# A clamp and a small addition move from VectorE to GpSimd in an attention and gated-MLP kernel

## The chip, the cores and the metric

The kernel runs on one core of a Trainium2 chip. The metric is the device time of one execution in microseconds (us), as a median of runs. The core has five engines with a queue each: TensorE (PE; its weight loads are listed as PEld), VectorE (DVE), ScalarE (ACT), GpSimd (POOL) and SyncE (SP, which issues the transfers). Each engine takes its instructions in the order in which they stand in its queue; a semaphore holds an instruction until what it needs is done.

## The reference

```python
mask   = q_bucket[:, :, :, None] == k_bucket[:, :, None, :]   # sign bits of q @ proj, k @ proj (6 bits)
scores = np.where(mask, scale * q @ k^T, -1e9);  scores -= max(scores)
attn   = exp(scores);  attn = attn / (sum(attn) + 1e-9);  x = attn @ v      # 2 x 8 heads, 768 x 64
x = x as (1536, 512)
x = ((x @ w1) * (x @ w2) @ w3) @ w_out                        # first MLP, weights 512 x 1024, 1024 x 1024, 1024 x 512
out = (sigmoid(x @ w_gate) * (x @ w_val)) @ w_out2            # second MLP, 512 x 1536, 1536 x 512
```

q, k, v and proj come as float32; the seven weight matrices come as float64.

## The kernel before

Products are made of float32 operands split into a high and a low part: ScalarE rounds the high part, VectorE or GpSimd subtracts to get the low part, and TensorE does three matmuls for each product (`three`).

**Decode.** The float64 weights are turned into float32 on the chip, in 76 units of 128x512 values. `stage_next` issues the load of a unit (512 KB) from SP into a tile `st`. `decode` then takes the two 32-bit words of each value: ScalarE writes the magnitude of the high word, read as a float32, to `da` (L334) and a scaled low word to `dr` (L335); VectorE clamps the magnitude between two constants (L336), shifts and masks it (L337), puts the sign bit back (L338), and adds the low bits into the destination (L343, shown in the trace as a custom operation). The tiles `da` and `dr` have one buffer in each of two pools in turn during attention, and two buffers later.

**Attention.** 96 steps, six for each of 16 heads. In a step TensorE makes 128x768 scores (L466, L469); VectorE takes their negated maximum (L476, L477); ScalarE does the exponential and, as a by-product, the sum of the row, into one column of `su` (L487); TensorE transposes the result (L520), ScalarE and VectorE split it (L523, L524), and TensorE multiplies it with v (L537). When all six columns of `su` are there, `emit_rows` adds 1e-9 to them (L498), takes the reciprocal (L499), and sends the 128x6 values as a row to DRAM and back as a broadcast `rr` (two transfers from SP). GpSimd multiplies the head pair's output by it (`emit_scale`, L510). GpSimd also makes the splits of the next heads' q, k and v (`split`, L366 and L369).

**Filler.** Between the attention steps the kernel multiplies w3 by w_out into `wc` (`gen_fill`, L593) and starts the first MLP on the first 512 tokens (`gen_first`). Forty of the 76 decodes belong to these two. GpSimd makes the low halves of w_out (L588) and of the weights (`split_w`, L692).

**Order.** Everything up to here is collected first, and then `order_engines` writes out the order of each engine's queue by a list schedule: priorities from the step, a cost for each instruction, and a delay for each hop from engine to engine. For GpSimd the cost does not look at the operation:

```python
        if e == "Pool":
            return 60 + n * 2.3
...
            ("Pool", "Activation"): 75, ("Pool", "DVE"): 69, ("Pool", "PE"): 203}
```

For VectorE a tensor_scalar of n elements costs 69 + 0.52 n. Both in ns.

**The MLPs.** `moe` goes over 52 tiles of 512 tokens by 128 features: 24 matmuls into `pa` and `pb`, 12 into the accumulators `m`. The weights of the tile after next are split by ScalarE and GpSimd (`wah`, `wal`, `wbh`, `wbl`, L692), those of the second product by ScalarE and VectorE (`wth`, `wtl`). In the first 24 tiles the other 36 decodes run, one or two a tile. The order of this part is set by the framework's own scheduler, not by `order_engines`.

Of the kernel before, what the change touches and what calls it, by code (L numbers as in the profile page):

```python
# [16 lines left out]
ALU = mybir.AluOpType  # L17
# [6 lines left out]
F64_LO = 2.0 ** -15  # L24
F64_HI = 2.0 ** 17 - 2.0 ** -7
# [203 lines left out]
def lsh_attention_moe_moe2_kernel(  # L229
# [40 lines left out]
    dve = nc.vector  # L270
    pool = nc.gpsimd
# [6 lines left out]
    def f(ap):  # L278
        return ap.bitcast(F32)
# [30 lines left out]
    def stage_next():  # L310

        if units:
            dst, src = units.pop(0)
            alt[0] += 1
            other = late.get("mp") or (wp if "mw" not in late else dec)
            t = (other if alt[0] % 2 else dec).tile([P, CH], U64, tag="st", name="st", bufs=2)
            shp = dst.shape
            ld = sync.dma_start(out=t if len(shp) == 2 else t.rearrange("p (k f) -> p k f", k=shp[1]), in_=src)
            if "c0" in late and alt[0] == 4:
                Tiles.holds.append((ld.ins.name, late["c0"].name))  # L320
            staged.append((dst, t))

    def decode():


        stage_next()
        dst, t = staged.pop(0)
        w = t[:, :].bitcast(U32).rearrange("p (n t) -> p n t", t=2)
        lw, hw = w[:, :, 0], w[:, :, 1]
        alt[1] += 1  # L330
        tp, nb = (late["mp"], 2) if "mp" in late else (wp if "mw" not in late and alt[1] % 2 else dec, 1)
        a = tp.tile([P, CH], U32, tag="da", name="da", bufs=nb)
        r = tp.tile([P, CH], I32, tag="dr", name="dr", bufs=nb)
        act.activation(out=f(a), in_=f(hw), func=AF.Abs)  # L334
        act.activation(out=r, in_=lw, func=AF.Copy, scale=2.0 ** -29)  # L335
        dve.tensor_scalar(out=f(a), in0=f(a), scalar1=F64_LO, scalar2=F64_HI, op0=ALU.max, op1=ALU.min)  # L336
        dve.tensor_scalar(out=a, in0=a, scalar1=3, scalar2=0x3FFFFFFF, op0=ALU.logical_shift_left, op1=ALU.bitwise_and)  # L337
        dve.scalar_tensor_tensor(out=a, in0=hw, scalar=0xC0000000, in1=a, op0=ALU.bitwise_and, op1=ALU.bitwise_or)  # L338
        ai, ri = a.bitcast(I32), r
        if len(dst.shape) == 3:  # L340
            ai = ai.rearrange("p (k f) -> p k f", k=dst.shape[1])
            ri = ri.rearrange("p (k f) -> p k f", k=dst.shape[1])
        dve.tensor_tensor(out=dst.bitcast(I32), in0=ai, in1=ri, op=ALU.add)  # L343
# [135 lines left out]
    def emit_exp(g):  # L479
        h, t = divmod(g, NT)  # L480
        s = sc_t.pop(g)
        sm = sm_t.pop(g)
        if t == 0:
            su_t[h] = ap_.tile([P, NT], F32, tag="su", name=f"su{h}")
        e = ap_.tile([P, S], F32, tag="e", name=f"e{g}", bufs=3)
        e_t[g] = e
        act.activation(  # L487
            out=e.rearrange("p (a c) -> p a c", a=2), in_=s[:, :, :HS], func=AF.Exp,
            bias=sm[:, 1:2], scale=sm[:, 0:1], accum_out=su_t[h][:, t:t + 1],
        )  # L490
        if t == NT - 1:
            emit_rows(h)

    def emit_rows(h):

        su = su_t.pop(h)
        rs = ap_.tile([P, NT], F32, tag="rs", name=f"rs{h}")
        dve.tensor_scalar(out=su, in0=su, scalar1=1e-9, scalar2=None, op0=ALU.add)  # L498
        dve.reciprocal(out=rs, in_=su)  # L499
        row = drm.tile([1, S], F32, tag="row", name=f"row{h}")  # L500
        sync.dma_start(out=row.rearrange("o (p c) -> (o p) c", c=NT), in_=rs)
        if h % 2 == 0:
            rr_t[h // 2] = ap_.tile([P, S], F32, tag="rr", name=f"rr{h}", bufs=1)
        r0 = (h % 2) * D
        sync.dma_start(out=rr_t[h // 2][r0:r0 + D], in_=row.to_broadcast([D, S]))
# [49 lines left out]
    def gen_fill():  # L555
# [11 lines left out]
        for _ in range(3):  # L567
            stage_next()
        decode()
        decode()  # L570
        for i in range(NF1):
            t3 = [wp.tile([P, NF1, P], F32R, tag=f"t3{x}", name=f"t3{x}_{i}") for x in range(2)]
# [11 lines left out]
            for j in range(NF1):  # L584
                if i == 0:
                    decode()
                    act_copy(wo[0][:, j], wor[j])
                    pool.tensor_tensor(out=wo[1][:, j], in0=wor[j], in1=f(wo[0][:, j]), op=ALU.subtract)  # L588
                    yield
                elif i + 1 < NF1 and j in (2, 5):  # L590
                    decode()
                for n, (x, y) in enumerate(((0, 0), (0, 1), (1, 0))):
                    pe.matmul(acc, lhsT=t3[x][:, j], rhs=wo[y][:, j], start=(j == 0 and n == 0), stop=(j == NF1 - 1 and n == 2))  # L593
                if j % 2 == 1:
                    if j == NF1 - 1:
                        act_copy(wc[:, i], acc)
                    yield
# [327 lines left out]
```

## Time and profile before

| what | before |
|---|---|
| median of 3 runs | 856.51 us |
| lowest, highest | 855.91, 858.85 us |
| the profiled execution: time | 857.49 us |
| the profiled execution: span | 855.5 us |
| granted TensorE clock (share of full) | 0.996 |
| PE, DVE, ACT, POOL busy | 805.7, 592.3, 525.2, 283.5 us |

The span goes from the first to the last instruction; the time is that of the whole execution, 2 us more. Busy times are sums of an engine's instruction records. A record of TensorE, VectorE or ScalarE may overlap the next one of the same engine by a little, since the end of an instruction overlaps the start of the next.

### The profile page before, as it was taken

The page shows a single profiled execution, that of the slowest core. Times are in us where ns is not written, and L with a number is a line of the kernel's source. Part 1 is how long each engine was busy: PE and PEld are TensorE (multiplying, and loading weights), DVE is VectorE, ACT ScalarE, POOL GpSimd, SP SyncE. Part 2 cuts the span into 40 slices and gives each one's busy share as a digit, 9 for nine tenths or more (in the row PEclk, how much of TensorE's full clock was granted, in tenths as well). Part 3 has the DMA queues.
Part 4 walks back from the last instruction along what each step waited for, and adds up shares of the span by engine and source line. Part 5 has one row for each costly group of instructions (what it writes and reads, how often), then busy time and mean ns, then how long its engine had stood idle before and what let it go on. Part 6 is the DMA issues. An engine that isn't in the chain of part 4 may idle for free.

```text
span 855.5 us, 12210 instructions
## 1 busy us (share of the span) xinstructions
PE 805.7 (94%) x4272; PEld 681.2 (80%) x4272; DVE 592.3 (69%) x1059; ACT 525.2 (61%) x1024; POOL 283.5 (33%) x236
## 2 busy tenths in 40 slices
PE   4777999999979999999999999999999999999998
PEld 3656888889878889897788777778888888888886
DVE  5999999998889999999569999972222222222222
ACT  4778878887778988888347656663334433343331
POOL 1343323232325343227423342343333323333230
PEclk9999999999989999999999999999999999999999
DMA  7555555443334544323105433400000000010001
GB/s 223 150 172 173 147 135 128 123 105 99 84 110 104 161 112 124 81 59 109 49 10 172 162 124 128 144 1 1 1 0 26 26 1 0 1 50 1 0 1 49
DMA packets 44908, 71.54 MB, mean 84 GB/s; under 512 B 6128, under 2 KB 32752, under 8 KB 44848
## 3 DMA queue, kind: packets, MB, share of 16 engines
q1 hardware_dynamic: 44848, 70.78, 28.7%
q8 instruction: 33, 0.54, 0.3%
q14 instruction: 27, 0.22, 0.1%
HBM read 52.43 MB, written 3.19 MB: 65 GB/s over the span
## 4 chain that ended last, share of the span: by engine, by line
PE 56%; DVE 29%; ACT 7%; issue 5%; DMA 2%; SPq 0%; DVEq 0%; ACTq 0%
PE pa L698 12%; PE m L698 11%; PE pb L698 11%; DVE da L338 4%; DVE pt L524 4%; PE tp L520 3%; PE av L537 3%; DVE s L476 3%; PE p L698 3%; DVE da L336 3%; PE wacc L593 3%; PE s L466 2%; PE gps L401 2%; ACT e L487 2%; PE s L469 2%
## 5 line engine op out<-in xcount | busy, mean ns | idle before, releaser
L738 DVE TENSOR_TENSOR pb<-pb,a 128x512 f32<-128x512 f32 x52 | 36.1, 694 | 138.8 <-PE pb L698 134.8
L520 PE MATMUL tp<-idf,e 128*128 128x128 f32 x576 | 100.8, 275 | 3.0 <-DVE pt L524 1.5
L524 DVE TENSOR_TENSOR pt<-tp,pt 128x384 fp32r<-128x384 f32 x192 | 100.7, 547 | 3.4 <-ACT pt L523 2.2
L523 ACT ACTIVATE pt<-tp 128x384 fp32r<-128x384 f32 x192 | 89.8, 494 | 21.1 <-PE tp L520 19.9
L487 ACT ACTIVATE e<-s,sm 128x768 f32<-128x768 f32 x96 | 95.9, 1000 | 10.2 <-DVE sm L477 9.7
L698 PE MATMUL pa<-x,wah 128*128 128x512 f32 x320 | 99.9, 390 | 1.4 <-DVE x L681 1.4
L698 PE MATMUL pb<-x,wbh 128*128 128x512 f32 x320 | 98.7, 389 | 0.0
L692 POOL TENSOR_TENSOR wal<-xall,wah 128x512 fp32r<-128x512 f32 x36 | 48.3, 1341 | 148.8 <-ACT wah L276 132.1
L476 DVE TENSOR_REDUCE s<-s 128x1 f32<-128x768 f32 x96 | 91.5, 954 | 8.6 <-PE s L469 8.5
L520 PEld LDWEIGHTS tp<-idf,e 128*128 128x128 f32 x576 | 71.5, 141 | 15.2 <-DVE pt L524 3.0
L334 ACT ACTIVATE da<-st 128x512 f32<-128x512 f32 x76 | 51.2, 673 | 47.0 <-DVE w1r L343 21.5
L537 PE MATMUL av<-pt,spv 128*128 128x256 f32 x576 | 78.7, 287 | 0.6 <-DVE pt L524 0.5
L537 PEld LDWEIGHTS av<-pt,spv 128*128 128x128 f32 x576 | 72.1, 191 | 2.8 <-DVE pt L524 0.9
L466 PE MATMUL s<-ak,aq 128*128 128x384 f32 x192 | 63.1, 385 | 9.3 <-ACT e L487 7.3
L698 PEld LDWEIGHTS pa<-x,wah 128*128 128x128 f32 x320 | 60.1, 188 | 14.7 <-DVE x L681 2.2
L593 PE MATMUL wacc<-wo,t 128*128 128x512 f32 x192 | 68.5, 420 | 2.9 <-POOL wo L588 1.4
L698 PEld LDWEIGHTS pb<-x,wbh 128*128 128x128 f32 x320 | 60.1, 188 | 12.5
L338 DVE SCALAR_TENSOR_TENSOR da<-st,da 128x512 uint32<-128x512 uint32 x76 | 64.6, 850 | 0.4
L698 PE MATMUL pa<-x,wal 128*128 128x512 f32 x160 | 62.3, 389 | 0.0
L698 PE MATMUL pb<-x,wbl 128*128 128x512 f32 x160 | 62.2, 389 | 0.0
L469 PE MATMUL s<-bk,bq 128*128 128x384 f32 x192 | 57.6, 365 | 0.0
L276 ACT ACTIVATE wah<-xall 128x512 fp32r<-128x512 f32 x36 | 22.7, 631 | 56.6 <-PE pa L698 56.6
(159 smaller groups left out, 1910.2 us busy)
## 6 DMA issues: line engine op xcount, KB each, us to landing
st<-in_moe_w_dram SPq DMA_DIRECT2D x32, 512.0 KB, 3.9
st<-in_moe_w_out_dram SPq DMA_DIRECT2D x20, 512.0 KB, 3.3
st<-in_moe_w_gate_dram SPq DMA_DIRECT2D x12, 512.0 KB, 3.5
st<-in_moe_w_val_dram SPq DMA_DIRECT2D x12, 512.0 KB, 3.5
rawq<-in_q_dram SPq DMA_DIRECT2D x16, 192.0 KB, 2.5
rawk<-in_k_dram SPq DMA_DIRECT2D x16, 192.0 KB, 3.3
rawv<-in_v_dram SPq DMA_DIRECT2D x16, 192.0 KB, 2.4
bq<-aq SPq DMA_DIRECT2D x16, 192.0 KB, 2.6
```

Of the source, the lines that this page charges most:

```text
L334: act.activation(out=f(a), in_=f(hw), func=AF.Abs)
L338: dve.scalar_tensor_tensor(out=a, in0=hw, scalar=0xC0000000, in1=a, op0=ALU.bitwise_and, op1=ALU.bitwise_or)
L466: pe.matmul(s[:, half, :HS], lhsT=m["aq"][:, qs], rhs=m["ak"][:, ks], start=True, stop=False)
L469: pe.matmul(s[:, half, :HS], lhsT=m["bq"][:, qs], rhs=m["bk"][:, ks], start=False, stop=True)
L476: dve.tensor_reduce(out=one[:, 1:2], in_=s[:, :, :HS], op=ALU.max, axis=AX.XY, negate=True)
L487: act.activation(out=e.rearrange("p (a c) -> p a c", a=2), in_=s[:, :, :HS], func=AF.Exp, bias=sm[:, 1:2], scale=sm[:, 0:1], accum_out=su_ ...
L520: pe.transpose(ps[:, j * P:(j + 1) * P], e[:, c * P:(c + 1) * P], idf)
L523: act.activation(out=dh, in_=src, func=AF.Copy)
L524: dve.tensor_tensor(out=lo[:, g % 2, half * 3:half * 3 + 3], in0=src, in1=f(dh), op=ALU.subtract)
L537: pe.matmul(acc[:, :2 * P].rearrange("p (a t) -> p a t", a=2), lhsT=w, rhs=r[:, :, c], start=(c == 0 and i == 0), stop=(c == NT - 1 and i ...
L593: pe.matmul(acc, lhsT=t3[x][:, j], rhs=wo[y][:, j], start=(j == 0 and n == 0), stop=(j == NF1 - 1 and n == 2))
L698: mm = pe.matmul(ps, lhsT=lhs[x], rhs=rhs[y], start=start and n == 0, stop=stop and n == 2)
```

## The change

In `decode` the clamp of the magnitudes is given to GpSimd, with its two comparisons in the other order; in `emit_rows` the addition of 1e-9 is given to GpSimd, with a multiplication by 1.0 as a second operation. Nothing else differs; the costs in `order_engines` stay.

```diff
@@ decode
         act.activation(out=f(a), in_=f(hw), func=AF.Abs)
         act.activation(out=r, in_=lw, func=AF.Copy, scale=2.0 ** -29)
-        dve.tensor_scalar(out=f(a), in0=f(a), scalar1=F64_LO, scalar2=F64_HI, op0=ALU.max, op1=ALU.min)
+        pool.tensor_scalar(out=f(a), in0=f(a), scalar1=F64_HI, scalar2=F64_LO, op0=ALU.min, op1=ALU.max)
         dve.tensor_scalar(out=a, in0=a, scalar1=3, scalar2=0x3FFFFFFF, op0=ALU.logical_shift_left, op1=ALU.bitwise_and)
@@ emit_rows
-        dve.tensor_scalar(out=su, in0=su, scalar1=1e-9, scalar2=None, op0=ALU.add)
+        pool.tensor_scalar(out=su, in0=su, scalar1=1e-9, scalar2=1.0, op0=ALU.add, op1=ALU.mult)
         dve.reciprocal(out=rs, in_=su)
```

## Rows read from the trace of the kernel before

**Rows 1.** The page: busy times, and the chain that ended last by engine.
```profile
PE 805.7 (94%) x4272; PEld 681.2 (80%) x4272; DVE 592.3 (69%) x1059; ACT 525.2 (61%) x1024; POOL 283.5 (33%) x236
...
PE 56%; DVE 29%; ACT 7%; issue 5%; DMA 2%; SPq 0%; DVEq 0%; ACTq 0%
```

**Rows 2.** Busy time (instructions) of PE, PEld, DVE, ACT, POOL in three stretches.
```profile
20.00:412.00 392.00, 361.90 (x2333) 316.89 (x2332) 367.19 (x700) 314.37 (x658) 140.73 (x127) 0.99 0.44 120
412.00:570.00 158.00, 153.98 (x669) 124.50 (x668) 140.21 (x215) 95.72 (x171) 55.61 (x36) 1.00 0.33 105
570.00:856.00 286.00, 281.70 (x1242) 232.59 (x1240) 74.05 (x108) 106.09 (x180) 85.23 (x66) 1.00 0.03 12
```

**Rows 3.** The chain, shares of a stretch by line: 20 to 412, then 412 to 570.
```profile
by line: DVE pt L524 7.8%; PE tp L520 7.6%; PE av L537 7.1%; DVE s L476 6.5%; PE wacc L593 6.0%; issue 5.1%; PE s L466 5.0%; PE gps L401 4.9%; ACT e L487 4.7%; PE s L469 4.4%; PE p L698 3.6%; DVE da L338 3.5%; DVE da L336 3.2%; ACT pt L523 
...
by line: issue 16.0%; DVE da L338 14.0%; DVE da L336 7.8%; DVE da L337 7.7%; PE p L698 6.9%; DVE wtl L692 6.7%; DVE gl L741 5.8%; DVE xall L343 4.6%; PE pa L698 4.4%; DVE w1r L343 4.1%; PE y L698 3.6%; ACT da L334 3.4%; DVE pb L738 2.9%; DV
```

**Rows 4.** The chain after 570, in time: start, us, what.
```profile
574.41 2.72 PE pb L698 x12
```

**Rows 5.** Groups by form, VectorE, 20 to 412: busy us, mean ns.
```profile
L338 DVE SCALAR_TENSOR_TENSOR da<-st,da 128x512 uint32<-128x512 uint32 x40 | 32.0, 800 | 0.2
L337 DVE TENSOR_SCALAR da<-da 128x512 uint32<-128x512 uint32 x41 | 25.1, 613 | 0.2
L336 DVE TENSOR_SCALAR da<-da 128x512 f32<-128x512 f32 x40 | 23.9, 602 | 1.0 <-ACT da L334 0.9
L548 DVE TENSOR_TENSOR xall<-av,xu 64x256 f32<-64x256 f32 x48 | 19.9, 414 | 7.1 <-ACT xu L276 6.1
L498 DVE TENSOR_SCALAR su<-su 128x6 f32<-128x6 f32 x16 | 4.8, 303 | 1.7 <-ACT e L487 1.5
```

**Rows 6.** GpSimd and VectorE in order of time near 87: start, us, engine, line.
```profile
86.79 2.27 POOL L510 TENSOR_TENSOR xall<-xall,rr 128x768 f32<-128x768 f32 x1
...
87.30 2.03 DVE L337 TENSOR_SCALAR da<-da 128x512 uint32<-128x512 uint32 x1
...
89.39 0.41 DVE L336 TENSOR_SCALAR da<-da 128x512 f32<-128x512 f32 x1
89.72 0.68 DVE L338 SCALAR_TENSOR_TENSOR da<-st,da 128x512 uint32<-128x512 uint32 x1
```

**Rows 7.** Groups by form, VectorE, 412 to 570: busy us, mean ns.
```profile
L338 DVE SCALAR_TENSOR_TENSOR da<-st,da 128x512 uint32<-128x512 uint32 x35 | 31.9, 912 | 0.2
L337 DVE TENSOR_SCALAR da<-da 128x512 uint32<-128x512 uint32 x34 | 18.7, 551 | 0.4
L336 DVE TENSOR_SCALAR da<-da 128x512 f32<-128x512 f32 x34 | 17.5, 514 | 0.6
```

**Rows 8.** Single lines and tiles: duration ns min/median/max, first and last start.
```profile
L337 DVE TENSOR_SCALAR da<-da x76: 406/420/2033, 14.5 to 564.4; 128x512 uint32<-128x512 uint32 x76
L338 DVE SCALAR_TENSOR_TENSOR da<-st,da x76: 650/682/1791, 15.1 to 564.9; 128x512 uint32<-128x512 uint32 x76
L336 DVE TENSOR_SCALAR da<-da x76: 407/418/1532, 13.7 to 561.8; 128x512 f32<-128x512 f32 x76
L498 DVE TENSOR_SCALAR su<-su x16: 152/161/862, 43.4 to 382.0; 128x6 f32<-128x6 f32 x16
L524 DVE TENSOR_TENSOR pt<-tp,pt x192: 516/547/560, 29.2 to 386.8; 128x384 fp32r<-128x384 f32 x192
L366 POOL CAST spk<-rawk x14: 503/506/1388, 22.3 to 324.0; 128x384 fp32r<-128x384 f32 x14
L692 POOL TENSOR_TENSOR wal<-xall,wah x36: 1286/1291/2680, 542.4 to 827.9; 128x512 fp32r<-128x512 f32 x36
```

**Rows 9.** VectorE's busy time (instructions) of L343 alone, two stretches.
```profile
20.00:412.00 392.00, 30.19 (x39) 0.99 0.44 120
412.00:570.00 158.00, 31.12 (x36) 1.00 0.33 105
```

**Rows 10.** Who waited for whom, GpSimd, 412 to 570: total us, times, longest.
```profile
POOL wal L692 <- ACT wah L276: 47.1, 11, 6.5
```

## The prediction

> **What bounds the kernel now.** I read the page's busy shares and chain first. TensorE is busy for 94% of the span, which would end the matter if a busy matmul record meant a matmul at its peak, but the chain that ended last gives TensorE 56% and VectorE 29% [rows 1]. So I cut the span into three stages [rows 2]. From 570 us on TensorE runs alone: VectorE works 74 of 286 us, no decode is left, and nothing of the change can reach it. In the attention stage (20 to 412 us) VectorE is busy 367.2 of 392 us (94%) and TensorE 361.9. In the stage with the last decodes (412 to 570 us) VectorE is busy 140.2 of 158 us.
>
> The chain cut to these stages [rows 3] shows what to read: in attention VectorE's, TensorE's and ScalarE's lines alternate in small pieces, with the clamp (L336) at 3.2% of 392 us, 12.5 us; in the second stage the three longest named groups are VectorE's decode lines, the clamp among them with 7.8% of 158 us, 12.3 us. Together 24.8 us: the most that taking the clamp off the chain can give if nothing takes its place.
>
> TensorE stands close behind. In the last stage twelve matmuls take 2.72 us [rows 4], 0.227 us each; 668 of them in the second stage [rows 2] make 151.4 us of 158, so no more than 6.6 us is to be had there. In attention the share of the chain tells: 29% of 855.5 us is 248 us, all of it ahead of 570, thus some 43% of the time in which VectorE can bound at all.
>
> **What is removed.** In attention 40 clamps at a mean of 602 ns, and 16 additions to the sums at 303 ns [rows 5]. An instruction's record overlaps the next one's: a clamp begins at 89.39, lasts 0.41, and its successor begins at 89.72 [rows 6], so 0.08 us of each duration is not worth counting. 40 x (0.602 - 0.08) + 16 x (0.303 - 0.08) = 20.9 + 3.6 = 24.5 us of VectorE's queue. In the second stage 34 x (0.514 - 0.08) = 14.8 us [rows 7].
>
> These means are well above the medians (0.42 for a clamp, 0.16 for an addition [rows 8]), and why decides the case. At 86.79 GpSimd starts a multiply of 2.27 us; VectorE's L337, a one-input operation between SBUF tiles of 0.42 us median [rows 8], starts at 87.30 and takes 2.03, until just after GpSimd is done [rows 6]. The two engines take turns. L524, which reads PSUM, stays between 516 and 560 ns in 192 instances [rows 8]. The Trainium skill (SBUF — State Buffer, "SBUF: two separate sides") says the same as a rule: the two engines share a pair of ports, which goes to the one that came first for its whole instruction; this row agrees with it.
>
> **What is added.** No row shows a two-operation tensor_scalar on GpSimd. From below: its one-input cast of 128x384 takes 0.506 us (median), and 512/384 of that is 0.67. From above: its two-input operation on 128x512 takes 1.29 us [rows 8]. The clamp has one input, so I take it nearer to the cast: 0.75 us with delays; both ends are kept for the range. The addition of 128x6 lies between VectorE's 0.16 us and the cast; I take 0.2. GpSimd thus gains 40 x 0.75 + 16 x 0.2 = 33.2 us in attention, on top of 140.7 of 392, and 34 x 0.75 = 25.5 us on top of 55.6 of 158 [rows 2]: it stays far from full.
>
> What this gives back in turns: I count the three decode lines that stay on VectorE, since the clamps will run beside them, at their means against 0.42 us for L337 and 0.68 for the others (medians [rows 8]). In attention L337 loses 25.1 - 41 x 0.42 = 7.9, L338 4.8 and L343 3.7 us [rows 5, 9], together 16.4 us against GpSimd's 140.7 [rows 2]: 0.117 us for each us that GpSimd works. 33.2 x 0.117 = 3.9 us. In the second stage it is 4.4, 8.1 and 6.6 us [rows 7, 9], 19.1 against 55.6, 0.344 for each. 25.5 x 0.344 = 8.8 us. The price there is three times as high, since decodes and weight splits crowd together.
>
> New waits: VectorE's L337 now waits for GpSimd, and behind it in order wait the max of the next scores, the low halves (L524, L741) and with them TensorE. Also, after the addition, the reciprocal (L499) waits for GpSimd, and behind it on SP the row transfer, its broadcast, and whatever weight load stands next in SP's queue. What such a hop costs is bounded by those that VectorE has: at best the clamp's own wait for ScalarE, 0.9 us over 40 instances, 0.02 each; at worst L548's for ScalarE, 6.1 us over 48, or 0.13 each [rows 5]. I take 0.06, near the middle: 56 x 0.06 = 3.4 us, and 34 x 0.06 = 2.0 us. The wait for ScalarE's absolute value moves to GpSimd's queue, where the splits and casts of heads stand behind it; their idle time, 47 us in front of `wal` alone in the second stage [rows 10], hides the 0.75 us. If that cover is gone, the split of the next weights is late next, and TensorE after it.
>
> Net: attention 24.5 - 3.9 - 3.4 = 17.2 us of VectorE, second stage 14.8 - 8.8 - 2.0 = 4.0. At the bounds (clamp 0.67 or 1.29, addition 0.16 or 0.51, hop 0.02 or 0.13) attention gives 20.0 or 10.2, the second stage 6.3 or -4.7.
>
> How much of it is time: if relief falls evenly, the share of the chain says 0.4; if VectorE alone bounds, 1. TensorE's pieces in the chain are as long as VectorE's, so I take 0.5, near the low end. That gives 8.6 + 2.0 = 10.6 us. The order of the first stage is written anew by the list schedule, with 60 + 2.3 x 512 = 1238 ns for a clamp on GpSimd, above what I expect: it should place L337 late enough. I count nothing for the new order itself.
>
> The profiled execution has a span of 855.5 and a time of 857.49 us; the median is 856.51, 1.0 below. 855.5 - 10.6 = 844.9 of span, 846.9 for that execution, 845.9 beside the median: 846.
>
> **The rivals.**
> *All of the relief arrives (chance 0.13).* For it: VectorE at 94% and the 24.8 us of the clamp on the chain. Against: TensorE's equal share. 856.5 - 24.8 = 831.7 at the most, 832 to 843.
>
> *The turns eat it (0.14).* If a clamp takes 1.29 us, like a two-input operation, and the second stage's price, 0.344, holds in attention too, because the clamps come just where L337 and L338 stand, 74 x 1.29 x 0.344 = 32.8 us come back; with 5.4 us of hops, 39.3 - 38.2 leaves 1.1, half of it 0.6 us: 856, between 853.5 and 859. For it: L338's 912 ns in the second stage. Against: attention's 0.117, and the cast's 0.506 us [rows 8]. The Trainium skill (Perfetto Trace Analysis, "Optimizing Scalar/DVE Operations") warns of this: moving work between these two engines might not help, since a two-port operation of VectorE locks GpSimd out. By that rule alone the sum is no gain.
>
> *Slower, by waits at L337 (0.23).* GpSimd's queue is in order. If clamps come to stand behind a weight split, or behind a split that waits for ScalarE (up to 6.5 us [rows 10]), L337 stalls VectorE, which has 7% of idle time to spare. Per decode w us of waiting: 39.3 - 12.7 (turns) - 1.0 (the additions' hops) = 25.6 us stand against 74w, so from w = 0.35 on it is a loss. Half a split (1.29 / 2 = 0.65) in front of each clamp would give 0.5 x (25.6 - 48.1) = -11.3 us: 868, between 860 and 875. For it: the second stage's order is not the list schedule's. Against: hops of 0.02 to 0.13 now.
>
> That the change does not do what it says can be excluded but for the order: the two instructions name their engine.
>
> **How the numbers follow.** My forecast, half of the relief, has 0.50 and lies from 843 to 854 (half of the sum of the bounds, 13 and 3 us). With 0.13 below it, 0.14 around no change and 0.23 above, 838 to 865 leaves out half of the first rival and half of the third, 0.18. A measurement of this kernel tells 0.3% (2.6 us) from no change. Faster by more: 0.50 + 0.13 and the edge of the second rival, 0.64; within: 0.12; slower: 0.24.
>
> **What the profile after should show.** Clamps on GpSimd at 0.67 to 1.0 us; VectorE's busy time in attention lower by some 25 us and its end some 9 us earlier; L337's mean up where GpSimd works, L338 above 912 ns in the second stage; waits of L337 for GpSimd of a few us in all; the last stage unchanged at 2.72 us per twelve matmuls. Wrong would be a clamp above 1.3 us, waits for GpSimd of over 26 us in all, or an attention stage that ends no earlier although VectorE has time to spare, which would mean that TensorE or the order bound it.

## The result, and the profile after

| | before | after |
|---|---|---|
| median of 5 runs (lowest to highest) | 857.48 us (855.91 to 858.85) | 851.40 us (847.82 to 851.83) |
| the profiled execution: span, time | 855.5, 857.49 us | 849.0, 851.55 us |
| ratio after / before, 95% interval | | 0.9917 (0.9902 to 0.9932) |

The change gains 6.1 us by the medians (0.7%; 0.8% by the ratio); 10.6 were forecast. The page after, to be read against [rows 1]: busy times, then the chain by engine.

```profile
PE 806.6 (95%) x4272; PEld 685.3 (81%) x4272; DVE 567.4 (67%) x967; ACT 523.9 (62%) x1024; POOL 336.6 (40%) x328
...
PE 69%; DVE 18%; issue 6%; ACT 4%; DMA 3%; SPq 0%; DVEq 0%; ACTq 0%
```

VectorE loses 92 instructions and GpSimd gains 92 (76 clamps, 16 additions). VectorE's share of the chain falls from 29% to 18%, TensorE's rises from 56% to 69%. The three stretches after, with the columns of [rows 2] (behind the engines stand TensorE's granted clock as a share of full speed, the share of the DMA engines and GB/s):

```profile
20.00:412.00 392.00, 370.77 (x2373) 328.75 (x2372) 348.81 (x650) 317.03 (x664) 174.89 (x186) 0.98 0.45 121
412.00:570.00 158.00, 152.22 (x655) 121.38 (x654) 135.85 (x175) 95.13 (x171) 76.48 (x70) 1.00 0.32 100
570.00:849.00 279.00, 275.30 (x1215) 227.71 (x1213) 71.53 (x103) 102.69 (x173) 81.43 (x63) 1.00 0.03 12
```

In the same 392 us TensorE now gets 2373 matmuls done instead of 2333. VectorE's busy time falls by 18.4 us, and GpSimd's rises by 34.2 (33.2 were forecast). Fixed stretches hide where time is won, though, because after is ahead of before in each. So from here on I cut at the same work, on TensorE: the last matmul with v (L537, the end of attention), and the first accumulation into `m` (L698) of the ninth and of the 18th MLP tile. The first mark, as the line's summary of L537 (count, duration ns min/median/max, first and last start), before and after:

```profile
L537 PE MATMUL av<-pt,spv x576: 276/279/562, 37.9 to 389.1; 128*128 128x256 f32 x192
```

```profile
L537 PE MATMUL av<-pt,spv x576: 275/277/562, 38.7 to 383.0; 128*128 128x256 f32 x192
```

The other two marks in order of time (start, us, engine, line, then idle time before), before and after:

```profile
499.82 0.47 PE L698 MATMUL m<-gh,wth 128*128 128x512 f32 x1 [0.65 <-DVE x L761]
...
576.97 0.39 PE L698 MATMUL m<-wth,gh 128*128 128x512 f32 x1
```

```profile
490.42 0.47 PE L698 MATMUL m<-gh,wth 128*128 128x512 f32 x1 [1.07 <-DVE x L761]
...
570.42 0.39 PE L698 MATMUL m<-wth,gh 128*128 128x512 f32 x1
```

This gives four parts of the span: attention up to 389.1 or 383.0 (6.1 us won); the handover, up to the ninth tile, 110.7 or 107.4 (3.3 won); the main decode part, tiles 9 to 17, 77.2 or 80.0 (2.8 lost); the rest, 278.5 or 278.6. 6.1 + 3.3 - 2.8 - 0.1 = 6.5, the difference of the spans. The forecast was 8.6 in attention, and 2.0 in what is the second and third of these parts together.

The lines of the decode after: VectorE and GpSimd in 20 to 412 us, by form (busy us, mean ns, then idle time before), beside [rows 5]; then the same from 412 to 570, beside [rows 7].

```profile
L338 DVE SCALAR_TENSOR_TENSOR da<-st,da 128x512 uint32<-128x512 uint32 x41 | 32.7, 797 | 0.3
L337 DVE TENSOR_SCALAR da<-da 128x512 uint32<-128x512 uint32 x40 | 23.9, 598 | 0.0
...
L336 POOL TENSOR_SCALAR da<-da 128x512 f32<-128x512 f32 x39 | 27.2, 699 | 76.7 <-ACT da L334 75.7
```

```profile
L338 DVE SCALAR_TENSOR_TENSOR da<-st,da 128x512 uint32<-128x512 uint32 x34 | 32.5, 957 | 0.9
L337 DVE TENSOR_SCALAR da<-da 128x512 uint32<-128x512 uint32 x34 | 25.2, 741 | 0.5 <-POOL da L336 0.5
...
L336 POOL TENSOR_SCALAR da<-da 128x512 f32<-128x512 f32 x34 | 25.1, 737 | 50.8 <-ACT da L334 50.8
```

A clamp costs GpSimd 0.70 to 0.74 us. In attention the neighbours L337 and L338 are as long as before, and the third decode line, L343, takes 31.6 us instead of 30.2 [rows 9] for its 39 instances, so hardly any turns were added there; in the second stretch L337 grows from 551 to 741 ns, L338 from 912 to 957, and the 36 instances of L343 take 34.9 us instead of 31.1 [rows 9]. L337 waits for GpSimd once, for 0.5 us.

### The profile page after: what moved, and what is told of

It reads as the page before. It is cut to its first block, busy times and chain, and to the rows that moved or that the text cites. A ratio compares the mean times of both kernels' runs of the same rounds, so it can differ in the third digit from the quotient of the medians.

```text
span 849.0 us, 12225 instructions
## 1 busy us (share of the span) xinstructions
PE 806.6 (95%) x4272; PEld 685.3 (81%) x4272; DVE 567.4 (67%) x967; ACT 523.9 (62%) x1024; POOL 336.6 (40%) x328
## 4 chain that ended last, share of the span: by engine, by line
PE 69%; DVE 18%; issue 6%; ACT 4%; DMA 3%; SPq 0%; DVEq 0%; ACTq 0%
PE pa L698 12%; PE pb L698 12%; PE m L698 11%; PE av L537 6%; PE tp L520 6%; PE p L698 5%; PE wacc L593 4%; PE s L466 3%; DVE da L337 3%; PE s L469 3%; DVE da L338 3%; PE gps L401 2%; PE y L698 2%; DVE pt L524 2%; DVE s L476 1%
## 5 line engine op out<-in xcount | busy, mean ns | idle before, releaser
L738 DVE TENSOR_TENSOR pb<-pb,a 128x512 f32<-128x512 f32 x52 | 36.2, 695 | 138.8 <-PE pb L698 134.8
L336 POOL TENSOR_SCALAR da<-da 128x512 f32<-128x512 f32 x76 | 54.1, 712 | 137.3 <-ACT da L334 136.3
L692 POOL TENSOR_TENSOR wal<-xall,wah 128x512 fp32r<-128x512 f32 x36 | 46.9, 1302 | 137.9 <-ACT wah L276 137.9
L698 PE MATMUL pa<-x,wah 128*128 128x512 f32 x320 | 98.9, 389 | 0.0
L698 PE MATMUL pb<-x,wbh 128*128 128x512 f32 x320 | 98.5, 389 | 0.0
L537 PE MATMUL av<-pt,spv 128*128 128x256 f32 x576 | 79.5, 289 | 0.2 <-DVE pt L524 0.2
L537 PEld LDWEIGHTS av<-pt,spv 128*128 128x128 f32 x576 | 73.5, 194 | 2.6 <-DVE pt L524 0.6
L466 PE MATMUL s<-ak,aq 128*128 128x384 f32 x192 | 63.7, 389 | 10.4 <-ACT e L487 8.9
L593 PE MATMUL wacc<-wo,t 128*128 128x512 f32 x192 | 70.5, 427 | 0.5 <-ACT wo L276 0.2
L698 PEld LDWEIGHTS pb<-x,wbh 128*128 128x128 f32 x320 | 60.1, 188 | 12.4
L698 PEld LDWEIGHTS pa<-x,wah 128*128 128x128 f32 x320 | 60.1, 188 | 12.4
L338 DVE SCALAR_TENSOR_TENSOR da<-st,da 128x512 uint32<-128x512 uint32 x76 | 65.9, 867 | 1.3
L698 PE MATMUL pb<-x,wbl 128*128 128x512 f32 x160 | 62.2, 389 | 0.0
L698 PE MATMUL pa<-x,wal 128*128 128x512 f32 x160 | 62.2, 389 | 0.0
```

The source lines that it names most:

```text
L336: pool.tensor_scalar(out=f(a), in0=f(a), scalar1=F64_HI, scalar2=F64_LO, op0=ALU.min, op1=ALU.max)
L466: pe.matmul(s[:, half, :HS], lhsT=m["aq"][:, qs], rhs=m["ak"][:, ks], start=True, stop=False)
L537: pe.matmul(acc[:, :2 * P].rearrange("p (a t) -> p a t", a=2), lhsT=w, rhs=r[:, :, c], start=(c == 0 and i == 0), stop=(c == NT - 1 and i ...
L698: mm = pe.matmul(ps, lhsT=lhs[x], rhs=rhs[y], start=start and n == 0, stop=stop and n == 2)
```

## The experiments

The theory after the result: VectorE's relief is what was won in attention; in the decode part the turns with GpSimd gave more back than was won. Rivals: the list schedule's new order, not the relief, made the gain; waits for GpSimd ate the rest; the addition, not the clamp, did one or the other. All times of one kernel below are medians, each against before as it ran beside it (856.96 to 857.56 us).

**The two edits alone.**

```diff
 sums_only:
-        dve.tensor_scalar(out=su, in0=su, scalar1=1e-9, scalar2=None, op0=ALU.add)
+        pool.tensor_scalar(out=su, in0=su, scalar1=1e-9, scalar2=1.0, op0=ALU.add, op1=ALU.mult)
 clamp_only:
-        dve.tensor_scalar(out=f(a), in0=f(a), scalar1=F64_LO, scalar2=F64_HI, op0=ALU.max, op1=ALU.min)
+        pool.tensor_scalar(out=f(a), in0=f(a), scalar1=F64_HI, scalar2=F64_LO, op0=ALU.min, op1=ALU.max)
```

> Only the addition to the sums on GpSimd, the clamp on VectorE as before. Theory 1 (VectorE is relieved, TensorE takes over the chain, so half of the relief is time): 16 additions of 0.30 us leave VectorE, some 3.6 us, half of it 1.8 at the most, less the new hop in front of the reciprocal: 0 to 2 us faster. Theory 2 (the new order of the list schedule moves the time, not the relief): any change of up to 4 us either way. Theory 3 (what VectorE gives up comes back as turns with GpSimd): no change.

> Only the clamp on GpSimd, the addition on VectorE as before. Theory 1: nearly the whole gain of the change, 5 to 7 us. Theory 2: not the same as the whole change, since the order is another again; off by 2 us or more. Theory 3: no gain.

sums_only: 859.81, ratio 1.0030 (1.0018 to 1.0042), 2.5 us slower. clamp_only: 848.56, 0.9902 (0.9887 to 0.9916), 8.8 us faster. Together -6.3, and the whole change is -6.1: the clamp is the gain, the addition a loss. The loss is not in attention, where the additions are: it ended at 385.9 in sums_only, earlier than before, and then the handover took 114.4 us instead of 110.7.

**The clamp in one stage only.** Of the 76 decodes, 40 run before the MLPs and 36 in them.

```diff
 clamp_attention (clamp_mlps: the other way round):
+        if "mp" in late:
+            dve.tensor_scalar(out=f(a), in0=f(a), scalar1=F64_LO, scalar2=F64_HI, op0=ALU.max, op1=ALU.min)
+        else:
+            pool.tensor_scalar(out=f(a), in0=f(a), scalar1=F64_HI, scalar2=F64_LO, op0=ALU.min, op1=ALU.max)
```

> The clamp on GpSimd in the 40 decodes of the attention stage alone, on VectorE in the 36 of the MLPs; the addition on VectorE. Theory 1, with what the profile of the change shows: the attention stage gains 6 to 9 us and the 2.4 us that the later decodes lose are not paid, so 7 to 10 us faster than before and about 2 better than the whole change. Theory 3 (turns eat it): no gain here. Theory 2: gain anywhere from 2 to 8 us.

> The clamp on GpSimd in the 36 decodes of the MLPs alone, on VectorE in the 40 of attention; the addition on VectorE. The order of the attention stage is that of before. Theory 1 with the turns of the second stage: 2 to 3 us slower than before. As the prediction had it (relief 4.0, half of it time): 2 us faster. Theory 2: no change, since the list schedule's order is not touched.

clamp_attention: 853.61, 0.9960 (0.9945 to 0.9974). clamp_mlps: 858.84, 1.0020 (1.0010 to 1.0030). So -3.7 and +1.5 us, against -8.8 for both at once; 7 to 10 us had been expected of clamp_attention. The parts at the same marks show why that is no contradiction (us; the marks' lines were read as above, and the rest is 278.5 or 278.6 in every kernel):

| kernel | attention ends | handover | main decode part |
|---|---|---|---|
| before | 389.1 | 110.7 | 77.2 |
| after | 383.0 | 107.4 | 80.0 |
| sums_only | 385.9 | 114.4 | 78.0 |
| clamp_only | 382.0 | 106.3 | 80.1 |
| clamp_attention | 382.7 | 113.4 | 77.2 |
| clamp_mlps | 387.1 | 108.6 | 80.0 |
| no_clamp | 379.2 | 109.8 | 74.1 |
| one_buffer | 382.4 | 103.3 | 73.4 |

Attention and the main decode part each follow their own clamps: some 5 to 6 us won in the one, 2.8 lost in the other, whatever is done elsewhere. The handover follows neither. (clamp_mlps and, further down, spread_before run the attention of before and both ended it at 387.1, not 389.1: profiles of the same instructions in the same order differ by that much here. The profiled execution of clamp_mlps took 856.26 us, 2.6 below its median, so that its row of the table shows less loss than the median does.)

**What the handover holds.** TensorE and VectorE in clamp_attention, in order of time (start, us, engine, line; L684, L341 and L661 are L681, L338 and L658 of before).

```profile
401.68 0.61 PE L701 MATMUL pa<-x,wah 128*128 128x512 f32 x2
406.60 0.79 PE L701 MATMUL y<-gl,wh 128*128 128x512 f32 x1 [4.31 <-DVE gl L661]
407.19 0.63 PE L701 MATMUL y<-gh,wl 128*128 128x512 f32 x1
407.62 0.63 PE L701 MATMUL y<-gl,wh 128*128 128x512 f32 x1
...
401.30 1.77 DVE L341 SCALAR_TENSOR_TENSOR da<-st,da 128x512 uint32<-128x512 uint32 x1
403.00 2.95 DVE L684 TENSOR_TENSOR x<-xall,x 128x512 fp32r<-128x512 f32 x3
405.87 0.68 DVE L661 TENSOR_TENSOR gl<-p,gh 128x512 fp32r<-128x512 f32 x1
```

TensorE stood 4.3 us for one low half, `gl`, which came behind a decode step of 1.77 us and three other low halves in VectorE's queue. After the stand its matmuls came 0.43 us apart until 411.9, where they come 0.227 apart in [rows 4]; the granted clock of these 4.7 us was 0.50, the lower of its two levels, 1.2 GHz. In after the same `gl` ran earlier:

```profile
400.23 0.68 DVE L658 TENSOR_TENSOR gl<-p,gh 128x512 fp32r<-128x512 f32 x1
```

What this does to 30 us, with the columns of [rows 2], first in clamp_attention, then in after: 103 matmuls at a granted clock of 0.89, and 131 at 1.00.

```profile
401.00:431.00 30.00, 25.69 (x103) 20.70 (x102) 12.28 (x16) 8.00 (x14) 11.61 (x9) 0.89 0.07 21
```

```profile
401.00:431.00 30.00, 29.50 (x131) 24.08 (x130) 15.58 (x21) 11.34 (x20) 14.67 (x11) 1.00 0.12 36
```

sums_only has the same hole, 3.8 us for `gl`. I tried to take it away in clamp_attention by holding back the three low halves:

```diff
 attention_low_first (on clamp_attention):
-        split_x(1, x2[1], range(KC))
+        split_x(1, x2[1], range(1))
+        with tc.issue_after(late["gl", 5].ins):
+            split_x(1, x2[1], range(1, KC))
```

> The clamp on GpSimd in attention alone, as in clamp_attention, and in VectorE's queue three of the four splits of the next tokens' x are put behind the low half (gl) that TensorE waits for at the handover. In clamp_attention TensorE stood still there for 4.3 us and then went at half its clock for 5 us. If that hole is what kept clamp_attention from the gain of the change: 846 to 850 us, 4 us or more better than clamp_attention's 853.6. If the hole only moves to another place: 853 as before.

852.09, 0.9940 (0.9924 to 0.9956): not told apart from clamp_attention, whose interval overlaps; the handover took 112.8 us instead of 113.4, and TensorE still stood 3.3 us for `gl`. So the rows show the hole, but this edit did not take it away, and what in the order would is left open.

**The order alone.** The work of before, but the list schedule is told that a clamp costs VectorE 1 ns, which is how its plan sees VectorE once the clamp is gone.

```diff
 order_alone:
+        if i.name in Tiles.free:
+            return 1.0
...
+        cl = dve.tensor_scalar(out=f(a), in0=f(a), scalar1=F64_LO, scalar2=F64_HI, op0=ALU.max, op1=ALU.min)
+        Tiles.free.append(cl.ins.name)
```

> The work of the kernel before, on the same engines, but the list schedule is told that a clamp costs VectorE nothing (1 ns), so the order of every engine is written as if VectorE had been relieved. Theory 1: no gain; 0 to 5 us slower, because the true work does not fit the order. Theory 2 (the order made the gain): 4 us faster or more.

863.99, 1.0079 (1.0067 to 1.0091): attention ended at 393.5. A new order without the relief does not make the gain, so the rival falls as it was put. This order is not that of after, which also plans 1238 ns on GpSimd for each clamp, and the relief in the old order was not run; what the two do together stays open.

```diff
 true_cost (on the whole change):
-            return 60 + n * 2.3
+            return 200 + n * 0.8 if op == "InstTensorScalarPtr" else 60 + n * 2.3
```

> The whole change, and the list schedule counts a one-tensor operation of GpSimd at what the profile shows, 200 + 0.8 n ns (610 ns for a clamp, 205 for an addition) in place of 1238 and 74. Theory 1: the order is not what bounds; within 2 us of the whole change. Theory 2: the 1238 ns made the schedule place the later decode steps too late; 3 us or more better than the change.

849.51, 0.9913 (0.9901 to 0.9925), against 0.9917 for after: no difference that the intervals tell. That the schedule charged 1238 ns for a clamp of some 620 cost little, as forecast.

**Without the clamp, and with two.**

```diff
 no_clamp:
-        dve.tensor_scalar(out=f(a), in0=f(a), scalar1=F64_LO, scalar2=F64_HI, op0=ALU.max, op1=ALU.min)
 clamp_twice (on the whole change): the pool.tensor_scalar line of the clamp stands twice
```

> The clamp of the magnitudes is left out altogether, the addition stays on VectorE: relief without GpSimd. Theory 1: VectorE loses 39 us of work and gains no turns; in attention TensorE bounds, so the gain there is that of the change (6 to 9 us) and little more; in the second stage up to the 6.6 us that TensorE leaves. Together 10 to 15 us faster. If VectorE alone bounded attention: 20 us or more. Theory 2 (order alone): not more than the change itself.

> The whole change with the clamp done twice in a row on GpSimd (the second writes the same values again): GpSimd works 76 x 0.62 = 47 us more. Theory 1: attention, bounded by TensorE, loses 0 to 3 us of the gain; the second stage loses by turns at 0.34 us for each us of GpSimd, 34 x 0.65 x 0.34 = 7.5 us of VectorE and at least half of it as time. 3 to 7 us slower than the whole change. Theory 3: the whole gain and more is lost, slower than before. If neither waits nor turns matter: the same as the change.

no_clamp: 844.66, 0.9859 (0.9846 to 0.9871). It is the zero against which the clamp has a price on either engine. In attention VectorE's clamps cost 387.1 - 379.2 = 7.9 us (389.1 gives 9.9), GpSimd's 382.0 - 379.2 = 2.8 (383.0 gives 3.8). In the main decode part VectorE's cost 77.2 - 74.1 = 3.1 us and GpSimd's 80.0 - 74.1 = 5.9. These prices contain what the order of each kernel adds, since leaving the clamps out changes it too. By them a clamp on GpSimd is not free, and in the decode part it is dearer there than on VectorE.

clamp_twice: 855.99, 0.9991 (0.9980 to 1.0001). The second clamps cost 4.6 us against after, all of it and more in attention (394.0 instead of 383.0); the main decode part even fell to 73.4, where 7.5 us of turns had been expected for that stage. The list schedule also charges the second clamp 1238 ns, so its order and its work are not told apart by this run, and I draw nothing from it for attention. For the main decode part it says more, below.

**What the decode part is full of.** The main decode part as one stretch, with the columns of [rows 2], before and after:

```profile
499.80:577.00 77.20, 75.04 (x324) 60.23 (x325) 71.62 (x105) 49.10 (x89) 28.85 (x19) 1.00 0.30 96
```

```profile
490.40:570.40 80.00, 76.37 (x324) 60.15 (x325) 71.00 (x91) 48.62 (x88) 40.90 (x36) 1.00 0.31 99
```

The same 324 matmuls, 73.5 us at 0.227 each. VectorE is busy 71.6 of 77.2 us and 71.0 of 80.0, the last 11 or 12 us of either stretch being behind the start of the last decode's last step (565.6 and 558.4). Its lines, by form (busy us, mean ns, idle time before), before and after:

```profile
L338 DVE SCALAR_TENSOR_TENSOR da<-st,da 128x512 uint32<-128x512 uint32 x17 | 16.7, 984 | 0.2
L337 DVE TENSOR_SCALAR da<-da 128x512 uint32<-128x512 uint32 x17 | 10.6, 623 | 0.3
L336 DVE TENSOR_SCALAR da<-da 128x512 f32<-128x512 f32 x17 | 10.4, 613 | 0.5
L343 DVE CUSTOM_DVE_ANT_0 wc<-da,dr 128x1024 uint16<-128x1024 uint16 x8 | 7.0, 881 | 0.0
L741 DVE TENSOR_TENSOR gl<-pb,gh 128x512 fp32r<-128x512 f32 x10 | 6.8, 683 | 0.7 <-ACT gh L276 0.7
```

```profile
L338 DVE SCALAR_TENSOR_TENSOR da<-st,da 128x512 uint32<-128x512 uint32 x18 | 18.1, 1006 | 0.5
L337 DVE TENSOR_SCALAR da<-da 128x512 uint32<-128x512 uint32 x18 | 15.7, 872 | 0.5 <-POOL da L336 0.5
L343 DVE CUSTOM_DVE_ANT_0 wc<-da,dr 128x1024 uint16<-128x1024 uint16 x8 | 9.4, 1180 | 0.4
L741 DVE TENSOR_TENSOR gl<-pb,gh 128x512 fp32r<-128x512 f32 x10 | 6.8, 685 | 3.0 <-ACT gh L276 3.0
```

GpSimd works 12.1 us more, and L337 takes longer beside it (623 to 872 ns). The last addition does so into `wc` (881 to 1180) but not into `w1r` (1116 to 679, not shown). With that, and with one decode more in the stretch (19 against 18), VectorE's busy time falls by 0.6 us although 10.4 us of clamps have left it. Its idle time grows by 3.4 us (5.6 to 9.0), 2.3 of it in front of L741, for ScalarE's `gh`. TensorE does not pay for these: its own waits in the same stretch, before and after (total us, times, longest), are as long for `gl` in both.

```profile
PE m L698 <- DVE gl L741: 2.0, 4, 0.7
PE m L698 <- DVE x L761: 0.7, 1, 0.7
```

```profile
PE m L698 <- DVE x L761: 2.8, 3, 1.1
PE m L698 <- DVE gl L741: 1.9, 4, 0.8
```

The first wait for `x` (0.65 and 1.07) stands in front of the mark and outside the part. The other two of after are new, 1.7 us of the 2.8. L761 is the subtraction that makes the low half of the first MLP's result and reads the accumulator `m` that TensorE writes next. Both times it stood in VectorE's queue behind an instruction drawn out beside GpSimd: an L337 that began at 493.19 and took 1.51 us, beside a split from 492.75 to 494.42, and a `wtl` (L692) of 1.64 us, beside a split of 1.30 (start, us, engine, line, idle before):

```profile
561.87 1.64 DVE L692 TENSOR_TENSOR wtl<-w2r,wth 128x512 fp32r<-128x512 f32 x1
561.67 1.30 POOL L692 TENSOR_TENSOR wal<-xall,wah 128x512 fp32r<-128x512 f32 x1 [2.66 <-ACT wah L276]
```

The other kernels with two buffers and one clamp on GpSimd in this part (clamp_only, clamp_mlps, true_cost, cost_and_spread) also wait 1.1 to 1.7 us for `x` within it, while clamp_attention and spread_before do not at all; but sums_only, with the clamp on VectorE, waits 1.5.

The Trainium skill (SBUF — State Buffer, "SBUF: two separate sides") has the engine that comes second blocked for the whole of the other's instruction, where VectorE's is in a two-port mode or reads two SBUF inputs; these two agree, each ending 0.3 to 0.5 us after GpSimd's. Its Perfetto Trace Analysis ("Optimizing Scalar/DVE Operations") warns that moving work between these two engines might not help: in clamp_mlps it did not (+0.2%), in clamp_only it did (-1.0%).

A rival is untested: the framework's scheduler also orders VectorE's queue anew here. Between `pb` and `gl` of a tile three or four instructions, nearly all decode steps, stand in most tiles of before, one or two in after, and no run moved the clamp and kept the order.

If a VectorE full of decodes is the trouble, decodes that are spread over more time should help more than cheaper ones. Three kernels try it. The first two change how many decodes are called for in each tile, 26 tiles instead of 24 in an even row; the third leaves a decode in the MLPs one buffer of `da` and `dr` instead of two, so that the next can't begin before the last one's VectorE steps are done.

```diff
 spread_before (on before); cost_and_spread (the clamp on GpSimd, the schedule's cost of true_cost, and):
-        return 1 + n % 2 if n <= 24 else 0
+        return 36 * n // 26 - 36 * (n - 1) // 26 if n <= 26 else 0
 one_buffer (on clamp_only):
-        tp, nb = (late["mp"], 2) if "mp" in late else (wp if "mw" not in late and alt[1] % 2 else dec, 1)
+        tp, nb = (late["mp"], 1) if "mp" in late else (wp if "mw" not in late and alt[1] % 2 else dec, 1)
```

> The kernel before, with the 36 decodes of the MLPs spread over the first 26 tiles (1.38 a tile) in place of 24 (1.5 a tile). If VectorE, full with decodes and turns, is what TensorE loses 5.7 us to in that stage: 2 to 4 us faster than before. If the waits there come from the order alone: no change. If the later weights come too late: slower.

> The clamp on GpSimd everywhere, the addition on VectorE, the list schedule with the true cost of GpSimd's one-tensor operations, and the 36 decodes of the MLPs spread over 26 tiles. If VectorE's turns with GpSimd cost TensorE some 8 us in the second stage and spreading thins them out: 843 to 847 us, better than clamp_only (848.6) and true_cost (849.5). If not: 848 to 850.

> The clamp on GpSimd everywhere, the addition on VectorE (clamp_only), and the tiles da and dr of the decodes in the MLPs with one buffer each in place of two, so that a decode there begins only when the last has left. If the loss of the second stage comes from VectorE's queue being packed with decode steps that stand before the low halves, fewer decodes under way should give some of it back: 845 to 848 us, 1 to 3 better than clamp_only's 848.6. If the packing is not the cause, the longer chain of each decode only delays the weights: 849 to 853.

spread_before: 856.96, 1.0001 (0.9988 to 1.0014). cost_and_spread: 851.85, 0.9932 (0.9915 to 0.9949), no better than clamp_only. In the two the last decode's last step still began at 562.7 and 560.3 us (565.6 in before): the number called for in a tile did not set when they ran. one_buffer: 839.13 us (836.45 to 839.65), 0.9772 (0.9751 to 0.9793), 9.4 us below clamp_only and 18.4 below before; 845 to 848 had been expected. The last eight decodes, into `wc` (line summary), in after and in one_buffer:

```profile
L343 DVE CUSTOM_DVE_ANT_0 wc<-da,dr x8: 675/1036/1741, 536.2 to 558.4; 128x1024 uint16<-128x1024 uint16 x8
```

```profile
L343 DVE CUSTOM_DVE_ANT_0 wc<-da,dr x8: 692/694/1565, 587.2 to 623.8; 128x1024 uint16<-128x1024 uint16 x8
```

The main decode part of one_buffer, tiles 9 to 17 as above, and VectorE's L738 in it:

```profile
485.70:559.10 73.40, 73.40 (x325) 60.81 (x324) 50.01 (x70) 44.07 (x76) 32.68 (x31) 1.00 0.29 94
```

```profile
L738 DVE TENSOR_TENSOR pb<-pb,a 128x512 f32<-128x512 f32 x9 | 6.2, 694 | 11.6 <-PE pb L698 11.6
```

The chain of one_buffer from 380 to 600 us, by line:

```profile
by line: PE pb L698 29.7%; PE pa L698 29.7%; PE m L698 27.2%; PE p L698 7.5%; PE y L698 4.9%; PE av L537 1.1%
```

VectorE is busy for 50.0 of 73.4 us and TensorE, which waits for nothing, for all of it. L738 waits 11.6 us for TensorE, where before and after show no idle time in front of it. The chain is TensorE's alone. The decodes run 65 us longer, over a stretch in which VectorE had worked 74 of 286 us [rows 2], and the rest of the kernel is as long as before (278.6 us). Against before 6.7 us are won in attention, 7.4 in the handover and 3.8 in the main decode part. One buffer with the clamp still on VectorE was not run, so how much of the 9.4 us needs the clamp on GpSimd stays open.

clamp_twice reached the same 73.4 us with two buffers. Its last decode's last step began at 636.6 us. Its main decode part:

```profile
502.50:575.90 73.40, 73.40 (x325) 60.81 (x324) 51.72 (x71) 45.30 (x78) 42.06 (x45) 1.00 0.29 94
```

GpSimd is busy there for 42.1 us, more than the 40.9 of after, and TensorE lost nothing, with some 13 decodes in this part instead of 18 or 19. So GpSimd's busy time does not cost TensorE time by itself here; what one_buffer and clamp_twice have in common is fewer decode steps in VectorE's queue.

## Why the prediction was right, and where not

It was right in sign and near in size, 846 against 851.4, but the terms of the sum were off in both directions, and that they came out near is in part luck.

**The clamp's price.** 0.75 us with delays was taken; the means were 0.70 and 0.74. Right, and the rival in which it takes 1.29 us falls.

**Waits for GpSimd.** 5.4 us were counted. VectorE waited 0.5 us in L337, and in L499 this much in attention (total us, times, longest):

```profile
DVE rs L499 <- POOL su L498: 1.7, 2, 1.0
```

The rival of waits at L337 falls with it: GpSimd had idle time in front of the clamps, waiting for ScalarE (75.7 us in attention).

**Turns.** By the prediction's own measure, the three decode lines against their medians, they went from 16.4 to 17.0 us in attention, 0.6 more where 3.9 were counted, and from 19.1 to 30.7 in the second stage, 11.6 more where 8.8 were counted. VectorE's busy time in attention fell by 18.4 us where some 25 were to be seen, in a fixed stretch in which after is 6.1 us further.

**"How much of it is time ... so I take 0.5" failed in both stages.** In attention the net relief of 17.2 us became 4.7 us (the clamp alone: 382.4, the mean of clamp_only and clamp_attention, against clamp_mlps) to 6.1 (after against before): 0.28 to 0.36. The share of the chain had said 0.4, and I went above it without a row. Where the rest went is seen up to the end of attention: the columns of [rows 2], then two lines of VectorE by form, before and after.

```profile
0.00:389.10 389.10, 350.12 (x2280) 308.63 (x2281) 355.35 (x718) 307.76 (x646) 124.92 (x124) 0.99 0.47 127
L476 DVE TENSOR_REDUCE s<-s 128x1 f32<-128x768 f32 x96 | 91.5, 954 | 8.6 <-PE s L469 8.5
L548 DVE TENSOR_TENSOR xall<-av,xu 64x256 f32<-64x256 f32 x47 | 19.5, 414 | 7.0 <-ACT xu L276 6.1
```

```profile
0.00:383.00 383.00, 350.53 (x2282) 313.10 (x2283) 337.01 (x666) 307.83 (x647) 155.10 (x180) 0.96 0.48 131
L476 DVE TENSOR_REDUCE s<-s 128x1 f32<-128x768 f32 x96 | 91.9, 957 | 13.0 <-PE s L469 12.8
L548 DVE TENSOR_TENSOR xall<-av,xu 64x256 f32<-64x256 f32 x47 | 19.5, 415 | 12.2 <-ACT xu L276 11.5
```

VectorE was busy 18.3 us less for the same attention. A third of that, 6.1 us, became time; 12.2 us became idle time of VectorE (33.8 to 46.0), 9.6 of it in front of these two lines, which wait for TensorE's scores and ScalarE's `xu`. no_clamp shows the limit: with no clamp at all attention ends 3 to 4 us earlier still, no more. The prediction's stage ended at 412 us, not at the end of attention. There after is 10.2 us ahead (2365 matmuls have begun by 412.0 us before and by 401.8 after), near the 8.6. But clamp_attention was 10.3 ahead there too and kept 3.3 by 431, so this lead is not the relief's alone.

In the decode part the factor had the wrong sign: 2.8 us were lost where a part of the 2.0 was expected. Most of the relief of 14.8 us went into the 11.6 of longer decode lines, which the rival "the turns eat it" had said. What TensorE then paid, by the rows, are its waits for `x` behind such instructions; the sum priced VectorE's waits for GpSimd (2.0 us) and not TensorE's for VectorE's low halves. That these are the cause of the 2.8 us is read from the rows, and no run took them away alone.

**"I count nothing for the new order itself" failed too.** The handover gained 3.3 us with the whole change and 4.4 with the clamp alone, and lost 2.7 in clamp_attention and 3.7 in sums_only, where `gl` came late. The addition to the sums was counted as a relief of 3.6 us; alone it costs 2.5. The total came out near by luck: the handover's gain, which no term had, stood in for what the other two terms lacked.

**The last stage.** The chain behind the decodes after, to be read against [rows 4]: unchanged.

```profile
573.30 2.72 PE pa L698 x12
```

## What to carry to other kernels

Before an instruction is moved off a full engine, cut the trace at the same work (not at the same times) and ask of each part how far the next engine stands behind; here the share of the chain (0.4) was nearer than a round half up to the end of attention, and still too high. Where background work fills the in-order queue of an engine that another one waits for, less background work in flight can help more than cheaper background work: one buffer instead of two gained 9.4 us on top of the clamp's 8.8. Parts of a change that are tried alone need not add up when a scheduler orders the queues anew at a seam between stages.

## What was unexpected in the hardware

GpSimd's clamp is fast: the duration of the two lines that moved to it, in after, over the whole span (ns, min/median/max).

```profile
L336 POOL TENSOR_SCALAR da<-da x76: 603/621/1083, 9.3 to 553.8; 128x512 f32<-128x512 f32 x76
...
L498 POOL TENSOR_SCALAR su<-su x16: 201/202/753, 43.3 to 377.2; 128x6 f32<-128x6 f32 x16
```

Two operations with constants on 512 columns take 0.62 us, the rate of its one-input cast (0.506 for 384 columns, [rows 8]) or a little better, and half of its two-input subtraction (1.29). And the stand of TensorE of 4.3 us in clamp_attention was followed by half as much again: the matmuls from 407.2 to 411.9 us came 0.43 us apart instead of 0.227, at a granted clock of 0.50, which is 2.2 us more for these 4.7.
